# More attention tiles transposed on VectorE, and two steps moved ahead, in a fused top-k attention and GELU MLP kernel

## The chip, the cores and the metric

One core of one Trainium2 chip runs the whole program. The metric is the device time of one execution in microseconds (us), less is better; the median of some runs stands for a kernel. The engines of the core are TensorE (PE, with its weight loads as PEld), VectorE (DVE), ScalarE (ACT), GpSimd (POOL) and SyncE, whose queue (SP) issues the DMAs here. Each runs its own instructions in program order and waits on semaphores for the others.

## The reference

Attention over 8 batches and 8 heads, 576 positions of 64 values, in which each query keeps only its 32 largest scores; then an MLP over the 4608 tokens. All is 32-bit float.

```python
scores = q @ k.transpose(0, 1, 3, 2) / np.sqrt(D)
kth = np.partition(scores, -32, axis=-1)[..., -32:-31]
scores = np.where(scores >= kth, scores, -1e9)
attn = np.exp(scores - scores.max(-1)); attn /= attn.sum(-1) + 1e-9
x = (attn @ v), heads side by side      # 4608 x 512
h = x @ w_in                            # 512 -> 2048
out = (0.5 * h * (1 + erf(h / np.sqrt(2)))) @ w_out
```

## The kernel before, in words

**Items and rings.** The attention is cut into 144 items. An item is 128 query rows of a pair of heads, so its scores are 128 × 1152 (two heads of 576 keys). A batch has 18 items: sixteen main ones (four pairs with four blocks of 128 rows) and two tail items for the last 64 rows of each head. `RINGS` is 36, the items of two batches; a ring of the loop is 36 iterations, and what an item gets is often decided by its number modulo 36. Below, n≡13 means an iteration whose number is 13 modulo 36.

**One iteration.** The loop over n works on several items at once. It issues the scores of n+2 and n+3 (L408, with the last 64 keys as the small matmul L373), the products P·V of item n−3 (`attend`, L742), ScalarE's selection and exponentials of n−1 (`select` L538, `softmax` L550), the transposes of P of n−2 (`transposes`, L657 and L671, copied out of PSUM by L660 and L686), the 32 largest of each row of n on VectorE (`top_k`: rounds of MAX8, L504, and MATCH_REPLACE, L507), and pieces of the MLP, which `room_in(n)` deals out to the iterations: first layer L811, second layer L929 to L967. Order within each engine is the order in which these calls are made.

**The top 32.** MAX8 gives 8 values of a row at a time. To shorten the first rounds, a row of 576 is folded to two halves of 288: the larger of each pair on VectorE (`larger`, L443), the smaller by an integer sum on POOL (`sum_up`, L468) less the larger (`smaller`, L476). Both lie in a tile "lists", of which there are two. The call of `larger(n+1)` stands at the start of iteration n, so on VectorE it follows the end of `top_k(n−1)`.

**From threshold to weights.** When the last MAX8 of item n has run, POOL turns the 32nd value into two biases (`threshold`, L518 and L519), ScalarE selects with the first one (L538, twice) and takes exponentials with the second (L550, twice, which also sums the row). POOL adds 1e-9 to the sums (`add_small`, L531), VectorE takes the reciprocal (`inverse`, L525, called as `last` at the end of the next `top_k`), and POOL multiplies the row by it (`normalise`, L573).

**Two ways to turn P.** P·V needs P with keys on partitions. The common way is nine 128 × 128 transposes on TensorE (L657 once, L671 eight times) and two copies on ScalarE. A *squared* item (`squared(i)`) goes another way: VectorE transposes it in 32 × 32 squares in place (`square_p`, L605, in the middle of the `top_k` two iterations later), SP writes it to DRAM by four DMAs (`write_p`, L615) and reads it back by four others in the turned order (`read_p`, L625). Before the change 66 items are squared: from 27 on, the even ones except 12 modulo 36, most tail items, and the odd ones that are 3, 13 or 25 modulo 36 (`LATER`, `moved(i)`).

**What "moved" brings.** A moved item i is attended at n = i+4 instead of i+3 (`mid`, `mids()`), since the way through DRAM takes longer. Its product uses the pair of PSUM banks "pr", of which there is one, shared with the scores and with the transposes "tp" of L671. `bare` in `room_in` shifts two MLP pieces by one iteration. Where the product's copy into xT (L747, by ScalarE) stands is decided around L1285: for an item in `starts_next` (1 modulo 36) ahead of the exponentials, for the others behind the first of them. Another bank, "z", serves by turns the product "seven" of the second layer (L965, copied by L983 or L986), the tail transposes and last keys ("t_ps", "tp_t").

**ScalarE in an odd iteration**: the two selects L538, a table load and the gelu (L827), the copy of "seven", a table load and the exponentials.

Of the kernel before, what the change touches and what calls it, by code (L numbers as in the profile page):

```python
# [14 lines left out]
def kernel(  # L15
# [19 lines left out]
    nc = tc.nc  # L35
    f32, i32, u32 = mybir.dt.float32, mybir.dt.int32, mybir.dt.uint32
    bf16, i16, u16 = mybir.dt.bfloat16, mybir.dt.int16, mybir.dt.uint16
    AF = mybir.ActivationFunctionType
    ALU = mybir.AluOpType

    B, H, S, D = q.shape
    P = 128
# [20 lines left out]
    work = ctx.enter_context(tc.tile_pool(name="work", bufs=2))  # L63
# [46 lines left out]
    def flush():  # L110
        held[0] = False
        while late_issues:
            late_issues.pop(0)()
        late_issues.extend(later)
        later.clear()
# [142 lines left out]
    for b in range(B):  # L258
# [4 lines left out]
        last = [(b * NP + p, NM) for p in range(0, NP, 2)]  # L263
# [13 lines left out]
    few = [False]  # L277
# [151 lines left out]
    lists_of = {}  # L429
    HS = S // 2  # L430

    def paired(i):

        return PAIRED <= i < N and i not in SINGLE

    def halves_of(i):
        s = S_of[i].rearrange("p (e h n) -> p e h n", e=2, h=2)
        return s[:, :, 0], s[:, :, 1]

    def larger(i):  # L440

        if paired(i):
            nc.vector.tensor_tensor(lists_of[i][:, :, 0], *halves_of(i), op=ALU.max)  # L443

    def into_of(i):

        if i < 2 and i not in into_lists:
            into_lists[i] = work.tile([P, 2, 2, HS], f32, tag="pt", bufs=1, name="into")
        return into_lists.get(i, lists_of[i])
# [3 lines left out]
    def first_lists():  # L453
# [6 lines left out]
        nc.gpsimd.tensor_tensor(both, a.bitcast(i32), top, op=ALU.subtract)  # L460
        nc.gpsimd.tensor_tensor(both, both, b.bitcast(i32), op=ALU.add)

    def sum_up(i):

        if paired(i):
            lists_of[i] = t = work.tile([P, 2, 2, HS], f32, tag="lists", name="lists")
            a, b = halves_of(i)
            nc.gpsimd.tensor_tensor(  # L468
                t[:, :, 1].bitcast(i32), a.bitcast(i32), b.bitcast(i32), op=ALU.add
            )  # L470
# [7 lines left out]
    def top_k(i, last, middle):  # L478


        stat_of[i] = st = {
            "first": work.tile([P, 2, 8], f32, tag="first", name="first"),
        }
        stat = work.tile([P, 4, 2], f32, tag="stat", name="stat")
        st.update((n, stat[:, x]) for x, n in enumerate(("neg", "bias", "den", "rden")))
        top = work.tile([P, 2, 16], f32, tag="top", bufs=1, name="top")
        into = [st["first"]] + [
            top[:, :, 8:16] if r == TOPK // 8 - 1 else top[:, :, 0:8] for r in range(1, TOPK // 8)
        ]
        if paired(i):  # L490
            t = lists_of[i]
            u = into_of(i)
            both = u.rearrange("p e h n -> p e (h n)")
            rounds = [(t[:, :, 0], u[:, :, 0]), (u[:, :, 0], u[:, :, 0])]
            rounds = [(*(rounds[r] if 16 * r < TOPK else (both, both)), x) for r, x in enumerate(into)]
        else:
            s = S_of[i].rearrange("p (e n) -> p e n", e=2)
            t = work.tile([P, 2, S], f32, tag="lists", name="rest")
            rounds = [(s if r == 0 else t, t, x) for r, x in enumerate(into)]
        for r, (src, dst, x) in enumerate(rounds):  # L500
            if 16 * r == TOPK:
                middle()
            for e in range(2):
                nc.vector.max(x[:, e], src[:, e])  # L504
            if r < len(rounds) - 1:
                for e in range(2):
                    nc.vector.match_replace(dst[:, e], x[:, e], src[:, e], LOWEST)  # L507
            if r == len(rounds) - 1:
                last()

        st["kth"] = top[:, :, 15]
# [9 lines left out]
    def inverse(i):  # L521
        if i < 0 or i >= N:
            return
        st = stat_of[i]
        nc.vector.reciprocal(st["rden"], st["den"])  # L525
# [17 lines left out]
    def softmax(i, e):  # L543

        if i < 0 or i >= N:
            return
        st, s = stat_of[i], row(i, e)
        if (i, e) not in selected:
            select(i, e)
        nc.scalar.activation(  # L550
            s, s, func=AF.Exp, bias=st["bias"][:, e : e + 1], scale=1.0,
            accum_out=st["den"][:, e : e + 1],
        )
# [23 lines left out]
    def squared(i):  # L577

        if not SINGLE.stop - 2 < i < N - 2:
            return False  # L580
        if items[i][1] == NM:
            return i % RINGS != RINGS // 2 - 1
        return moved(i) or (i % 2 == 0 and i % RINGS != 12)

    LATER = (3, 13, 25)

    def moved(i):

        return RINGS <= i < N - 8 and i % RINGS in LATER

    def delayed(i):

        return squared(i) and items[i][1] == NM
# [4 lines left out]
    RINGS = 2 * len(items) // B  # L598
    turned = {}

    def square_p(i):

        if squared(i):
            s = S_of[i]
            nc.vector.transpose(s, s)  # L605

    def write_p(i):

        if squared(i):
            turned[i] = d = dram.tile([SQ, NJ + NM, P // SQ, P], f32, tag="turned", name="turned")  # L610
            s = S_of.pop(i).rearrange("p (x j) -> p x j", j=SQ)
            d = d.rearrange("i c k n -> i (c k) n")
            for a in range(P // SQ):
                rows = slice(a * SQ, (a + 1) * SQ)
                nc.sync.dma_start(out=d[:, :, rows], in_=s[rows])  # L615
# [498 lines left out]
    def mlp(n):  # L1114
        for _ in range(n):
            if done[0] >= len(pieces) or pieces[done[0]][0] > ready[0] or left[0] == 0:
                return
            pieces[done[0]][1]()
            done[0] += 1
            left[0] -= 1  # L1120
            if eager[0]:
                run_gelus()
                run_small(9)
# [33 lines left out]
    for pair in range(2):  # L1157
        for piece in transpose_qk(pair, pair == 0):
            piece()
        if pair == 0:  # L1160
            scores(0)
            first_lists()
            scores(1)
            sum_up(1)
# [28 lines left out]
    starts_next = [x + 1 for x in starts]  # L1193
    sums_in = {START + 8 + j: j for j in range(FT // 2)}
    ahead = N + 4
    for n in range(ahead):

        held[0] = n < N and squared(n - 2)
        mid = [i for i in (n - 5, n - 4) if delayed(i) and n % 2 and (i % 2 or i in starts)]
        if moved(n - 4):  # L1200
            mid = [n - 4]
# [9 lines left out]
        def mids():  # L1211
            attend(mid.pop(0))
            if not mid:
                copy_x()
                read_p(n - 3)
                issue_soon()
# [7 lines left out]
        if n > 0:  # L1224
            larger(n + 1)
# [57 lines left out]
            softmax(n - 1, 1)  # L1283
        if few[0]:
            room = ODD if n % 2 else 0  # L1285
            if mid and mid[0] in starts_next:
                mlp(1)
                mids()
                room -= 1
            if n % 2 or not ahead_of_x:  # L1290
                softmax(n - 1, 0)
            if mid:
                mlp(1)
                mids()
                room -= 1
            if n % 2 and ahead_of_x:
                softmax(n - 1, 1)
            mlp(room)
# [35 lines left out]
        mlp(left[0])  # L1334
        run_gelus()
        if n < N:
            top_k(n, lambda: inverse(n - 1), lambda: square_p(n - 2))
            write_p(n - 2)
            flush()
            if n == 0:  # L1340
                larger(1)
        else:
            inverse(n - 1)
        threshold(n)
        if n == 0:
            smaller(1)
        normalise(n - 1)
        sum_up(n + 2)
        if n in sums_in:
            weight_sums(sums_in[n])  # L1350
# [56 lines left out]
```

## Time and profile before

| | |
|---|---|
| median of 3 runs | 1465.61 us (1465.57 to 1466.32) |
| the profiled execution | 1466.12 us, of which its span is 1464.0 |
| TensorE busy | 1444.8 us (99%), 8639 matmuls |
| VectorE busy | 1323.7 us (90%) |
| ScalarE busy | 1060.0 us (72%) |
| POOL busy | 1138.0 us (78%) |
| DMA | 134.13 MB, 92 GB/s on average |

A row of the time line reads: start (us from the start of the span), duration (us), engine, line, operation, tile written <- tiles read, shapes, how many such in a row; in brackets the idle time just before on that engine and what ended it. In the groups stand the total busy time and the mean of one in ns. In the waits stand who waited for whom, the total, how often, and the longest.

### The profile page before, as it was taken

The numbers are of one execution on the slowest core, as the hardware profiler recorded it, in microseconds if no ns is written. First come the engines' busy times: TensorE is split into PE (matmuls) and PEld (weight loads), VectorE is DVE, ScalarE is ACT, GpSimd is POOL, SyncE is SP. The second block draws the span as 40 slices with busy tenths as digits, with TensorE's granted clock in tenths as the row PEclk, the third lists the DMA queues.
The fourth block names the chain that finished last, engine by engine and source line by source line (L and its number), as shares of the span: only waits on it lengthen the run. The fifth ranks groups of instructions, "written<-read, shape, count | busy, mean of one in ns | idle before, by whom it ended". The sixth has DMA issues, their size and how long they took to land. (4 is left out here: it accounts for less than half of the span.)

```text
span 1464.0 us, 26591 instructions
## 1 busy us (share of the span) xinstructions
PE 1444.8 (99%) x8639; PEld 1126.5 (77%) x8639; DVE 1323.7 (90%) x3337; ACT 1060.0 (72%) x1887; POOL 1138.0 (78%) x1290
## 2 busy tenths in 40 slices
PE   8999999999999999999999999999999999999999
PEld 6776677877777777787777778787777777787887
DVE  7999899999999999999999999999999999999701
ACT  7999977876777777767777777776776767677620
POOL 6877667877897879877898878887788887978632
PEclk9999999999999999999999999999999999999999
DMA  7524310045454446455454365455555443643300
GB/s 193 152 87 124 85 48 1 16 96 99 90 113 89 84 91 141 82 112 113 96 100 95 61 116 115 89 114 112 98 100 110 86 84 78 128 99 75 65 15 15
DMA packets 580043, 134.13 MB, mean 92 GB/s; under 512 B 494881, under 2 KB 571457, under 8 KB 579905
## 3 DMA queue, kind: packets, MB, share of 16 engines
q1 hardware_dynamic: 578640, 132.01, 42.6%
q8 instruction: 68, 1.11, 0.3%
q14 instruction: 71, 0.57, 0.1%
q10 hardware_dynamic: 1200, 0.39, 0.1%
q0 software_dynamic: 64, 0.03, 0.0%
HBM read 84.01 MB, written 48.37 MB: 90 GB/s over the span
## 5 line engine op out<-in xcount | busy, mean ns | idle before, releaser
L811 PE MATMUL h_ps<-xT,w_in_sb 128*128 128x256 f32 (+1 forms) x2560 | 533.2, 361 | 0.0
L811 PEld LDWEIGHTS h_ps<-xT,w_in_sb 128*128 128x128 f32 x2560 | 438.2, 190 | 70.3 <-issue 11.3
L504 DVE MAX8 top<-lists 128x8 f32<-128x576 f32 (+1 forms) x792 | 475.0, 638 | 0.0
L507 DVE MATCH_REPLACE8 lists<-top,lists 128x288 f32<-128x288 f32 (+1 forms) x528 | 307.4, 587 | 0.0
L538 ACT ACTIVATE s<-s,stat 128x576 f32<-128x576 f32 x288 | 217.8, 778 | 113.4 <-POOL stat L518 113.2
L573 POOL TENSOR_TENSOR s<-s,stat 128x1152 f32<-128x1152 f32 x135 | 286.3, 2121 | 0.3 <-DVE stat L525 0.3
L550 ACT ACTIVATE s<-s,stat 128x576 f32<-128x576 f32 x288 | 223.8, 780 | 7.6
L468 POOL TENSOR_TENSOR lists<-s 128x576 int32<-128x576 int32 x133 | 189.9, 1427 | 0.0
L476 POOL TENSOR_TENSOR lists<-lists 128x576 int32<-128x576 int32 x132 | 186.1, 1410 | 3.1
L742 PE MATMUL o<-pt,raw_v 128*64 128x256 f32 x1280 | 152.9, 384 | 1.5 <-issue 0.6
L416 ACT ACTIVATE s<-s_ps 128x1024 f32<-128x1024 f32 x127 | 125.0, 1032 | 39.6 <-PE s_ps L408 39.5
L531 POOL TENSOR_SCALAR stat<-stat 128x2 f32<-128x2 f32 x144 | 31.4, 218 | 153.7 <-ACT s L550 147.2
L742 PEld LDWEIGHTS o<-pt,raw_v 128*64 128x64 f32 x1280 | 87.4, 136 | 81.9 <-issue 38.9
L967 PE MATMUL y_ps<-w_out_sb,sum 128*128 128x256 f32 x472 | 140.4, 379 | 0.0
L408 PE MATMUL s_ps<-kt,qm 64*128 64x512 f32 x512 | 129.6, 619 | 0.8 <-ACT s L414 0.8
L827 ACT ACTIVATE g<-h_ps 128x512 f32<-128x512 f32 x144 | 78.2, 595 | 70.3 <-PE h_ps L811 69.7
L967 PE MATMUL y_ps<-w_out_sb,g 128*128 128x256 f32 x480 | 115.8, 381 | 0.0
L507 DVE MATCH_REPLACE8 lists<-first,lists 128x288 f32<-128x288 f32 x264 | 114.1, 437 | 0.0
L443 DVE TENSOR_TENSOR lists<-s 128x576 f32<-128x576 f32 x133 | 109.1, 821 | 4.4 <-ACT s L381 1.8
L504 DVE MAX8 first<-lists 128x8 f32<-128x288 f32 x268 | 106.3, 435 | 0.0
L967 PEld LDWEIGHTS y_ps<-w_out_sb,g 128*128 128x128 f32 x480 | 90.5, 190 | 14.4 <-issue 2.3
L967 PEld LDWEIGHTS y_ps<-w_out_sb,sum 128*128 128x128 f32 x472 | 89.7, 190 | 12.2
(162 smaller groups left out, 2373.4 us busy)
## 6 DMA issues: line engine op xcount, KB each, us to landing
turned<-s SPq DMA_DIRECT2D x264, 144.0 KB, 3.6
pt<-turned SPq DMA_DIRECT2D x264, 144.0 KB, 3.2
raw_v<-in_v_dram SPq DMA_DIRECT2D x64, 128.0 KB, 2.5
raw_q<-in_q_dram SPq DMA_DIRECT2D x112, 72.0 KB, 2.4
raw_k<-in_k_dram SPq DMA_DIRECT2D x112, 72.0 KB, 2.4
out_dram<-y SPq DMA_DIRECT2D x30, 256.0 KB, 3.1
w_out_sb<-in_moe_w_in_dram SPq DMA_DIRECT2D x14, 511.8 KB, 4.9
w_out_sb<-in_moe_w_out_dram SPq DMA_DIRECT2D x10, 511.8 KB, 4.0
```

The lines of the kernel that those rows point to most:

```text
L408: nc.tensor.matmul(s_ps[:, e], lhsT=q_t[rows, :], rhs=kt[rows, main_keys(pair)], start=True, stop=True)
L416: nc.scalar.activation(spread(s, S + TL, SM), s_ps, func=AF.Copy, scale=scale)
L468: nc.gpsimd.tensor_tensor(t[:, :, 1].bitcast(i32), a.bitcast(i32), b.bitcast(i32), op=ALU.add)
L476: nc.gpsimd.tensor_tensor(into_of(i)[:, :, 1].bitcast(i32), both, top, op=ALU.subtract)
L504: nc.vector.max(x[:, e], src[:, e])
L507: nc.vector.match_replace(dst[:, e], x[:, e], src[:, e], LOWEST)
L538: nc.scalar.activation(s, s, func=AF.Prelu, bias=st["neg"][:, e : e + 1], scale=1.0, alpha=STEEP)
L550: nc.scalar.activation(s, s, func=AF.Exp, bias=st["bias"][:, e : e + 1], scale=1.0, accum_out=st["den"][:, e : e + 1],)
L573: nc.gpsimd.tensor_tensor(s, s, wide, op=ALU.mult)
L742: nc.tensor.matmul(o[e * D : (e + 1) * D, 0:n], lhsT=vt[:, j, e, :], rhs=pt[:, e * NJ + j if j < NM else NM, :], start=(j == 0), stop=(j = ...
L811: nc.tensor.matmul(h_tile(u)[:, i, :], lhsT=w_in_sb[:, ko, f * P : (f + 1) * P], rhs=xT[:, ko, c0 : c0 + n], start=(ko == 0), stop=(ko == ...
L967: nc.tensor.matmul(acc[names][:, k], lhsT=lhsT, rhs=rhs, start=(j == 0 and k == 0), stop=(j == FT // 2 - 1 and k == 1),)
```

## The change

Three edits. `LATER` goes from three numbers to six, so that of the odd items those that are 1, 9 and 31 modulo 36 go by squares as well (eight items: 37, 45, 67, 73, 81, 103, 109, 117); since 3 stands first, `LATER[0]` is 3. The copy of the product of an item 3 modulo 36 is put ahead of the exponentials, like that of 1 modulo 36. And at the end of `top_k(n)` VectorE computes `larger(n+2)` ahead of the reciprocal of n−1, where before it came behind it; the tile "lists" is made by whichever comes first, `larger` or `sum_up`. The order of the instructions on TensorE is otherwise kept, but for the nine transposes of each of the eight items, their products, which move one iteration later, and two first-layer pieces around each.

```diff
+    have_larger = set()
+
     def larger(i):
 
-        if paired(i):
-            nc.vector.tensor_tensor(lists_of[i][:, :, 0], *halves_of(i), op=ALU.max)
+        if paired(i) and i not in have_larger:
+            have_larger.add(i)
+            nc.vector.tensor_tensor(lists_for(i)[:, :, 0], *halves_of(i), op=ALU.max)
...
+    def lists_for(i):
+
+        if i not in lists_of:
+            lists_of[i] = work.tile([P, 2, 2, HS], f32, tag="lists", name="lists")
+        return lists_of[i]
+
     def sum_up(i):
 
         if paired(i):
-            lists_of[i] = t = work.tile([P, 2, 2, HS], f32, tag="lists", name="lists")
+            t = lists_for(i)
...
-    LATER = (3, 13, 25)
+    LATER = (3, 1, 9, 13, 25, 31)
...
-            if mid and mid[0] in starts_next:
+            if mid and (mid[0] in starts_next or mid[0] % RINGS == LATER[0]):
                 mlp(1)
                 mids()
                 room -= 1
...
-            top_k(n, lambda: inverse(n - 1), lambda: square_p(n - 2))
+            def last():
+                if few[0]:
+                    larger(n + 2)
+                inverse(n - 1)
+
+            top_k(n, last, lambda: square_p(n - 2))
```

## The prediction, made before the result was known

> **What bounds the kernel now.** I read the page's head and engine sums first, then the windows of two whole rings (36 iterations each), then the waits grouped by what ended them, then the time line of single iterations.
>
> ```profile
> span 1464.0 us, 26591 instructions
> PE 1444.8 (99%) x8639; PEld 1126.5 (77%) x8639; DVE 1323.7 (90%) x3337; ACT 1060.0 (72%) x1887; POOL 1138.0 (78%) x1290
> ```
>
> ```profile
> 362.50:706.20 343.70, 342.00 (x2024) 266.96 (x2023) 331.00 (x838) 250.56 (x452) 285.78 (x322) 1.00 0.50 101
> 706.20:1050.40 344.20, 342.14 (x2025) 267.05 (x2025) 331.10 (x839) 250.53 (x452) 285.75 (x322) 1.00 0.51 101
> ```
>
> The columns are the stretch, its length, then the busy time of PE, PEld, DVE, ACT and POOL. TensorE is busy for 342.1 of 344.2 us at a granted clock of 1.00; VectorE for 331.1. So TensorE sets the time, but VectorE has only 13.1 us of room in a ring, and the waits say what that room is made of:
>
> ```profile
> DVE stat L525 <- POOL stat L531: 55.2, 68, 6.2
> ACT s L538 <- POOL stat L518: 113.2, 43, 6.1
> ```
>
> VectorE idles almost only ahead of its reciprocal (L525), which waits for POOL's small addition L531. And ScalarE waits for VectorE's last MAX8 through POOL's L518 before its two selects. In an odd iteration those selects stand ahead of two table loads, the gelu and the copy of "seven", whose bank the next last-keys matmul on TensorE takes. So TensorE follows VectorE's threshold there with a fixed lag. This iteration, n=43, shows it:
>
> ```profile
> 419.24 0.17 DVE L525 RECIPROCAL stat<-stat 128x2 f32<-128x2 f32 x1 [0.21 <-POOL stat L531]
> 419.29 0.22 POOL L518 TENSOR_SCALAR stat<-top 128x2 f32<-128x2 f32 x1
> 419.54 1.44 ACT L538 ACTIVATE s<-s,stat 128x576 f32<-128x576 f32 x2 [6.11 <-POOL stat L518]
> 423.26 0.38 ACT L986 COPY p<-seven 128x256 f32<-128x256 f32 x1
> 423.70 0.49 PE L373 MATMUL tp_t<-kt,qm 128*128 128x128 f32 x2
> 424.02 0.27 PE L657 MATMUL tp_t<-ident,s 128*128 128x128 f32 x1
> 424.13 0.60 PE L967 MATMUL y_ps<-w_sum,sum 128*128 128x256 f32 x2
> 425.73 0.35 ACT L747 COPY xT<-o 128x256 f32<-128x256 f32 x1
> ```
>
> From threshold to the end of the copy of "seven" go 4.35 us (423.64 − 419.29), and TensorE starts 0.06 us later: no slack. At n=41 (mod 36: 5) and n=73 (mod 1) the copy ends 0.99 and 1.08 us before TensorE comes; at n=59 and 61 (mod 23, 25) TensorE waits for it even now:
>
> ```profile
> 404.31 0.38 ACT L983 COPY y<-seven 128x256 f32<-128x256 f32 x1
> 405.68 0.27 PE L373 MATMUL t_ps<-kt,qm 128*128 128x128 f32 x1
> 710.38 0.38 ACT L986 COPY p<-seven 128x256 f32<-128x256 f32 x1
> 711.84 0.27 PE L373 MATMUL tp_t<-kt,qm 128*128 128x128 f32 x1
> ```
>
> ```profile
> 574.96 1.39 PE L753 MATMUL o<-pt,raw_v 128*64 128x64 f32 x40 [0.27 <-ACT p L986]
> 597.35 0.49 PE L373 MATMUL tp_t<-kt,qm 128*128 128x128 f32 x2 [0.27 <-ACT p L986]
> ```
>
> **The change part by part.** *Squares.* Items 37, 45, 67, 73, 81, 103, 109 and 117 become squared: 1, 9 and 31 of the rings, less 139, which is past the limit.
>
> ```profile
> L605 DVE STREAM_TRANSPOSE s<-s 128x1152 f32<-128x1152 f32 x66 | 89.9, 1362 | 0.0
> L686 ACT COPY pt<-tp 128x1024 f32<-128x1024 f32 x67 | 68.3, 1020 | 38.8 <-PE tp L671 37.8
> 1363.23 0.87 PE tp L671 x8
> ```
>
> Each takes from TensorE eight transposes of 0.87 us together (the chain's row) and the one of L657, 0.11 (424.02 to 424.13): 0.98, in all 8 × 0.98 = 7.8 us. ScalarE loses a 1.02 and a 0.25 us copy, off its path. VectorE gains 8 × 1.36 = 10.9 us. Each also issues four writes and four reads on SP's queue:
>
> ```profile
> pt<-turned SPq DMA_DIRECT2D x264, 144.0 KB, 3.2
> 421.98 2.53 SPq L625 DMA_DIRECT2D pt<-turned  x4
> ```
>
> The item behind each moved one is read only after the moved product, as 40 is at 421.98; its own product comes in the next iteration (9.55 us each, 343.7/36), so the 3.2 us lie under TensorE's work and cost nothing; without that cover they would cost up to 3.2 each, 25.6 in all. SP is otherwise idle here. Two first-layer pieces move by one iteration and cost nothing in sum.
>
> *Product copied early.* At n=43, 79 and 115 the eight L671 wait for L747, which stands behind an exponential (425.73 above):
>
> ```profile
> 426.13 1.09 PE L671 MATMUL tp<-ident,s 128*128 128x128 f32 x8 [0.97 <-ACT xT L747]
> ```
>
> The stall of some 1.14 us (with its weight load) goes: 3 × 1.14 = 3.4. If VectorE took no part, the sum would be −7.8 − 3.4 = −11.2.
>
> *Larger halves first.* In 116 iterations L443 goes ahead of the reciprocal. Where that waits for POOL at the end of ScalarE's exponentials (four places in a ring, as 545.50 below), VectorE gets 0.6 to 0.76 us; where POOL itself is late with L476 (n≡2, 10 and others), L476 and L443 cannot run at once, so I count 0.18. Whether the order costs anything shows in pairs of rows:
>
> ```profile
> 706.40 0.22 POOL L518 TENSOR_SCALAR stat<-top 128x2 f32<-128x2 f32 x1 [0.59 <-DVE stat L525]
> 706.42 0.78 DVE L443 TENSOR_TENSOR lists<-s 128x576 f32<-128x576 f32 x1
> 706.58 0.67 POOL L519 TENSOR_TENSOR stat<-top,first 128x2 f32<-128x2 f32 x1
> ```
>
> ```profile
> 564.46 0.76 DVE L443 TENSOR_TENSOR lists<-s 128x576 f32<-128x576 f32 x1
> 564.51 0.79 POOL L518 TENSOR_SCALAR stat<-top 128x2 f32<-128x2 f32 x1 [0.58 <-DVE stat L525]
> ```
>
> ```profile
> 685.50 2.11 POOL L573 TENSOR_TENSOR s<-s,stat 128x1152 f32<-128x1152 f32 x1
> 685.77 2.45 DVE L443 TENSOR_TENSOR lists<-s 128x576 f32<-128x576 f32 x1 [0.62 <-ACT s L381]
> ```
>
> Where POOL's L518 starts 0.02 us ahead of L443 it takes 0.22 and L519 is held; where L443 starts 0.05 us ahead, L518 takes 0.79; where POOL's L573 is at work, L443 takes 2.45 instead of 0.76. Now the reciprocal's 0.15 us let L518 in first. Without it, L443 starts about 0.15 us ahead of L518 nearly everywhere, and the threshold comes at the end of L443: 0.79 − 0.22 = 0.57 later, less about 0.1 as L443 starts in the reciprocal's place: an estimate of **+0.47 us** on every select, the value of the nearest row; bounds 0 (as at 706.40) and 0.57.
>
> The Trainium skill, "SBUF — State Buffer", section "Who interferes with whom", says that a VectorE instruction with two SBUF inputs and a GpSimd instruction that reads SBUF exclude each other, and that whichever issues first holds the other off entirely. By it every one of the 116 would pay; the rows at 564.46 and 685.77 agree, and 706.42 differs, where the one issued 0.02 us later lost only 0.02.
>
> *How these meet.* TensorE can keep its gain only where VectorE's threshold is not what it waits for. VectorE is set back to TensorE's pace at n≡2 and 10, where POOL's sums wait for the second layer's products:
>
> ```profile
> 725.61 0.17 DVE L525 RECIPROCAL stat<-stat 128x2 f32<-128x2 f32 x1 [1.04 <-POOL stat L531]
> 796.05 0.73 POOL L848 TENSOR_TENSOR sum<-g 128x256 f32<-128x256 f32 x1 [2.12 <-PE y_ps L967]
> 801.35 0.17 DVE L525 RECIPROCAL stat<-stat 128x2 f32<-128x2 f32 x1 [1.68 <-POOL stat L531]
> 545.50 0.17 DVE L525 RECIPROCAL stat<-stat 128x2 f32<-128x2 f32 x1 [1.43 <-POOL stat L531]
> ```
>
> From n≡2 to 8: VectorE has one more transpose and the later threshold, less 0.18 at n≡2 and some 0.25 of the short waits between (0.21 at 419.24): +1.36 + 0.47 − 0.18 − 0.25 = +1.4. TensorE has −0.98. They meet at "seven" of n≡5 and 7: 1.4 + 0.98 = 2.4 us of waiting, part of it put off from 5 to 7 by the slack of 0.99. With the gain of 0.98 and the old stall of 1.14 gone, 2.4 − 0.98 − 1.14 = **+0.3**.
>
> From n≡10 to 13: VectorE +1.36 + 0.47 − 0.18 = +1.65, TensorE −0.98. At n≡13 item 9's product is now copied behind the first exponential, in the pair of banks that the transposes take:
>
> ```profile
> 476.57 0.22 POOL L518 TENSOR_SCALAR stat<-top 128x2 f32<-128x2 f32 x1 [0.58 <-DVE stat L525]
> 482.61 1.04 PE L671 MATMUL tp<-ident,s 128*128 128x128 f32 x8
> 482.93 0.19 ACT L550 ACTIVATION_READ_ACCUMULATOR s<-s,stat 128x1 f32 x1
> ```
>
> Here the copy would begin at 483.02 and end at 483.37 (6.80 after L518; 6.79 at n=43), where TensorE came at 482.61: 0.76 + 1.65 + 0.98 = 3.4 us of waiting, **+2.4** after the gain of 0.98.
>
> From 13 to 25 the rows that wait 0.27 lose their cause in part, since VectorE fills its waits there: **−0.3** (bounds −0.9 and 0). From 25 to 2: −0.98 for item 31, of which the pin at n≡1 (slack 1.08) leaves **−0.1** (bounds −0.98 and +0.5). Sum: 0.3 + 2.4 − 0.3 − 0.1 = +2.3 a ring, in three **+7.0 us**.
>
> The profiled execution took 1466.12 us, 2.1 outside its span; the median of the runs, 1465.61, is 1.6 over the span. 1464.0 + 7.0 + 1.6 is about 1472.5.
>
> **The rivals.** *A, the forecast*: VectorE's threshold sets TensorE's pace. For it: lags with 0.06 and no slack; against it: that the places are few. 1468.5 to 1477, by the bounds of its terms (0.2 to 0.57 of delay, the last two stretches at either end).
>
> *B, TensorE alone sets the time*: 1464.0 − 11.2 + 1.6 = 1454.4. For it: 99% busy, and VectorE's 13.1 us of room a ring against 8 × 1.36 = 10.9 in three. Against it: that room stands ahead of L525, mostly at places other than those where the transposes are put. It decides in favour of B if the tp of n≡13 comes more than 6.8 us after L518, against 6.04 now (482.61 − 476.57) less what TensorE saves.
>
> *C, no delay from L443's order* (L518 still gets through): 0.47 a meeting goes, VectorE keeps its fills, and the sum per ring is −0.5 to 0, about 1464. For it: 706.42, where 0.02 us decided in POOL's favour. Part-way to B the stall at n≡13 shrinks while item 31 keeps its 0.98: 1457 to 1462.
>
> *D, worse*: the pin at n≡1 holds back all of item 31's gain and n≡13's wait carries through to 25, with nothing given back: 3 × (0.3 + 2.4 + 0.5) = 9.6 and more, over 1476. The change not doing what it says: L443 first is issued in all 116 places, so only its benefit can fail, which is C or A.
>
> **How the numbers follow.** A 0.5 (1472.5), C 0.2 (1464), B 0.13 (1454.4), between B and C 0.07, D 0.1. A run of this kernel tells about 0.2% from no change, 2.9 us: faster is under 1462.7. B and the part-way case with a little of C make faster 0.22; C and A's lower edge make same 0.18; the rest of A and D make slower 0.60. The range goes from 1457 to 1477 and leaves out most of B and D. A's own range is 1468.5 to 1477.
>
> **What would show it.** Right: eight L671 that wait for L747 at n≡13 for some 3 us three times (and none at n≡7); "seven" waited for at n≡5 and 7 by 1 to 2 us each; L518 at 0.7 to 0.8 us in most rows. TensorE's busy sum falls by 7.8, VectorE's rises by some 11. B is shown by a span that falls with TensorE's sum; C by L518 at 0.22 behind L443. The forecast is wrong if VectorE's reciprocal still waits as long in a ring as now.

## The result, and the profile after

| | before | changed |
|---|---|---|
| median of 7 runs, us | 1466.0 (1464.96 to 1467.45) | 1470.4 (1469.86 to 1472.59) |
| ratio | | 1.0034, 95% interval 1.0023 to 1.0045 |
| span of the profiled execution | 1464.0 | 1468.4 |

The change makes the kernel 4.4 us slower: on the side of the forecast, whose size was +7.0. The page of the changed kernel, its head and engine sums:

```profile
span 1468.4 us, 26543 instructions
PE 1441.6 (98%) x8567; PEld 1119.6 (76%) x8567; DVE 1337.1 (91%) x3345; ACT 1049.9 (71%) x1871; POOL 1129.4 (77%) x1290
```

The 72 transposes are gone from TensorE (8639 to 8567), and eight instructions more run on VectorE (3337 to 3345), busy for 13.4 us longer. TensorE's share has fallen: it waits. (Its busy sum fell by 3.2 us, not by the 7.8 that the transposes were to save.) Its waits, in total, times, longest (L373 is unmoved, L680 was L671, L756 was L747, L992 and L995 were L983 and L986, L751 was L742):

```profile
PE tp_t L373 <- ACT y L992: 3.5, 3, 1.2
PE tp L680 <- ACT xT L756: 2.9, 3, 1.0
PE tp_t L373 <- ACT p L995: 2.8, 6, 0.6
...
PE t_ps L373 <- ACT y L992: 1.7, 2, 1.2
PE o L751 <- DMA turned<-s: 1.1, 1, 1.1
```

The waits for the copy of "seven" (L992, L995) are new but for the short ones at n=59 and 61. The wait of the transposes for the product's copy has the same total as before, 2.9, and yet is another: it is gone from n≡7 and has come to n≡13. The time line of n=49 shows both, from the threshold (L527, L518 before) on:

```profile
477.93 0.22 POOL L527 TENSOR_SCALAR stat<-top 128x2 f32<-128x2 f32 x1 [0.53 <-DVE top L513]
477.95 0.78 DVE L446 TENSOR_TENSOR lists<-s 128x576 f32<-128x576 f32 x1
...
482.34 0.49 PE L373 MATMUL tp_t<-kt,qm 128*128 128x128 f32 x2 [1.16 <-ACT y L992]
...
484.78 0.33 PE L680 MATMUL tp<-ident,s 128*128 128x128 f32 x1 [0.97 <-ACT xT L756]
```

The threshold stands 1.36 us later than before (477.93 against 476.57), the copy of "seven" behind it begins at 481.91, and TensorE, which had saved its transposes, waits 1.16 us there and 0.97 us once more for the product. At n=41 and 43 it waits for "seven" alone (the bank is "t_ps" at n=41):

```profile
406.22 0.49 PE L373 MATMUL t_ps<-kt,qm 128*128 128x128 f32 x2 [1.17 <-ACT y L992]
...
425.11 0.49 PE L373 MATMUL tp_t<-kt,qm 128*128 128x128 f32 x2 [0.60 <-ACT p L995]
```

How far TensorE is behind the kernel before can be read at the start of one and the same scores matmul (L408) in both traces:

| place (start before, us) | ring 1 | ring 2 | ring 3 |
|---|---|---|---|
| ahead of n≡2 | −0.21 (371.1) | 1.36 (696.9) | 2.20 (1041.1) |
| behind n≡7 | 0.22 (429.8) | 1.65 (772.7) | 2.50 (1116.8) |
| behind n≡13 | 2.24 (524.2) | 3.07 (888.3) | 4.52 (1212.1) |
| behind n≡25 | 2.23 (601.3) | 3.12 (945.5) | 4.57 (1289.0) |
| end of the ring, item 31 done | 1.36 (696.9) | 2.20 (1041.1) | 4.44 (1347.0), no item 31 |

So the loss has one place: the stretch to n≡13 costs 2.0, 1.4 and 2.0 us, and n≡2 to 7 some 0.3 to 0.4; where item 31 is squared 0.9 comes back.

### The profile page after: what moved, and what is told of

It reads as the page before. It is cut to its first block, busy times and chain, and to the rows that moved or that the text cites. A ratio compares the mean times of both kernels' runs of the same rounds, so it can differ in the third digit from the quotient of the medians.

```text
span 1468.4 us, 26543 instructions
## 1 busy us (share of the span) xinstructions
PE 1441.6 (98%) x8567; PEld 1119.6 (76%) x8567; DVE 1337.1 (91%) x3345; ACT 1049.9 (71%) x1871; POOL 1129.4 (77%) x1290
## 5 line engine op out<-in xcount | busy, mean ns | idle before, releaser
L582 POOL TENSOR_TENSOR s<-s,stat 128x1152 f32<-128x1152 f32 x135 | 284.8, 2110 | 8.6 <-DVE stat L534 3.4
L485 POOL TENSOR_TENSOR lists<-lists 128x576 int32<-128x576 int32 x132 | 186.6, 1414 | 3.1
L540 POOL TENSOR_SCALAR stat<-stat 128x2 f32<-128x2 f32 x144 | 44.1, 306 | 164.6 <-ACT s L559 152.6
L751 PE MATMUL o<-pt,raw_v 128*64 128x256 f32 x1280 | 152.9, 384 | 2.5 <-DMA turned<-s 1.1
L751 PEld LDWEIGHTS o<-pt,raw_v 128*64 128x64 f32 x1280 | 87.9, 136 | 79.2 <-issue 38.3
L408 PE MATMUL s_ps<-kt,qm 64*128 64x512 f32 x512 | 129.6, 619 | 0.8 <-ACT s L414 0.8
L446 DVE TENSOR_TENSOR lists<-s 128x576 f32<-128x576 f32 x133 | 106.2, 799 | 17.4 <-ACT s L381 6.0
L614 DVE STREAM_TRANSPOSE s<-s 128x1152 f32<-128x1152 f32 x74 | 101.1, 1366 | 0.0
```

Of the source, the lines that this page charges most:

```text
L408: nc.tensor.matmul(s_ps[:, e], lhsT=q_t[rows, :], rhs=kt[rows, main_keys(pair)], start=True, stop=True)
L485: nc.gpsimd.tensor_tensor(into_of(i)[:, :, 1].bitcast(i32), both, top, op=ALU.subtract)
L582: nc.gpsimd.tensor_tensor(s, s, wide, op=ALU.mult)
L751: nc.tensor.matmul(o[e * D : (e + 1) * D, 0:n], lhsT=vt[:, j, e, :], rhs=pt[:, e * NJ + j if j < NM else NM, :], start=(j == 0), stop=(j = ...
```

## The experiments

Times are the median less that of the kernel before on the same chip (1466.07, 1466.52 and 1466.09 for the three sets). The interval is that of the ratio.

| run | us against before | ratio |
|---|---|---|
| changed kernel | +4.4 | 1.0034 (1.0023 to 1.0045) |
| e1 no new squares | −2.1 | 0.9986 (0.9977 to 0.9994) |
| e2 larger halves behind | +4.7 | 1.0033 (1.0021 to 1.0045) |
| e3 new squares free | −1.2 | 0.999 (0.9981 to 0.9999) |
| e4 early copy for 9 | +2.7 | 1.0019 (1.001 to 1.0028) |
| e6 only 9 | +1.7 | 1.0015 (1.0006 to 1.0024) |
| e8 early copy alone | −4.0 | 0.9974 (0.9963 to 0.9984) |
| e9 free, early copy for 9 | −1.3 | 0.9992 (0.9983 to 1.0001) |
| e10 early copy and 31 | −5.1 | 0.9964 (0.9952 to 0.9976) |
| e11 early copy, 1 and 31 | −0.9 | 0.9994 (0.9985 to 1.0003) |
| e12 the same, free | −5.1 | 0.9966 (0.9953 to 0.9978) |
| e13 early copy, 9 free | 0.0 | 0.9999 (0.999 to 1.0007) |
| e16 early copy, 21 and 31 | +1.4 | 1.0008 (0.9999 to 1.0016) |

**e1: the squares taken out.**

```diff
-    LATER = (3, 1, 9, 13, 25, 31)
+    LATER = (3, 13, 25)
```

> The changed kernel without the eight new squared items: the larger halves ahead of the reciprocal and the early copy stay. Theory P (VectorE's threshold sets TensorE's pace, and the eight transposes on VectorE are what it cannot bear): the stall of 1.14 us at n=43, 79 and 115 goes and little comes back, so 2 to 5 us under the kernel before. Rival O (the new order on VectorE is what costs, since POOL's small instructions are held off while L446 runs): 1 to 5 us above the kernel before, close to the changed kernel.

2.1 us under the kernel before: the loss is the squares'. But the early copy alone gives 4.0 (e8), so the reordering costs 1.9 here.

**e2: the reordering taken out.**

```diff
             def last():
-                if few[0]:
-                    larger(n + 2)
                 inverse(n - 1)
```

> The changed kernel with the larger halves behind the reciprocal again; the eight squares and the early copy stay. Theory P: the transposes cost as before and VectorE can no longer fill its waits for the reciprocal, so 0 to 6 us above the changed kernel (4 to 10 us above the kernel before). Rival O: the delays of POOL's small instructions go, and the time falls to within 2 us of the kernel before or under it.

4.7 us over the kernel before, the same as the changed kernel within the intervals. Rival O falls for the kernel with the squares. What is striking is VectorE's wait for POOL ahead of its reciprocal, in e2 and then in the changed kernel:

```profile
DVE stat L534 <- POOL stat L540: 54.4, 68, 6.2
```

```profile
DVE stat L534 <- POOL stat L540: 29.7, 29, 6.2
```

The reordering takes 25 us off this wait, and the time stays. But most of the 25 us are not won. The idle time ahead of L446 itself (the last but one number of these rows, first e2, then the changed kernel) grows by 13.7 us:

```profile
L446 DVE TENSOR_TENSOR lists<-s 128x576 f32<-128x576 f32 x133 | 105.2, 792 | 3.7 <-ACT s L381 1.3
```

```profile
L446 DVE TENSOR_TENSOR lists<-s 128x576 f32<-128x576 f32 x133 | 106.2, 799 | 17.4 <-ACT s L381 6.0
```

VectorE's busy sum is 7.1 us larger as well (1330.0 in e2, 1337.1). Span less busy sum, its idle time goes from 137.8 to 131.3 us: 6.5 us less, not 25.

**e3: the new squares without VectorE's work.** The kernel leaves the eight transposes on VectorE out, so that eight items of P stay unturned; the rest of their way is kept.

```diff
-        if squared(i):
+        if squared(i) and not (moved(i) and i % RINGS in (1, 9, 31)):
             s = S_of[i]
             nc.vector.transpose(s, s)
```

> The changed kernel without the eight new transposes on VectorE; all else of the squares stays (the way through DRAM, the later products, nine transposes fewer on TensorE each), so eight items of P reach the product unturned. Theory P: with 8 x 1.36 us of VectorE gone TensorE keeps its 7.8 us and the 3.4 us of the early copy, but for a stall behind the product's copy at n=49, 85 and 121 of 1 to 1.5 us each: 5 to 9 us under the kernel before. Rival W (the later product, its pair of PSUM banks and the DMAs are what costs, VectorE's load is not): within 2 us of the changed kernel.

1.2 us under the kernel before, 5.6 under the changed one. VectorE's eight transposes are worth most of what was lost, which W denied; but theory P had 5 to 9 under the kernel before, and it missed: something else holds TensorE too. Of its waits there remain 2.6 us for the product's copy at n≡13, 2.4 for "seven", and this one:

```profile
PE o L751 <- DMA pt<-turned: 1.7, 2, 0.9
```

It is the way through DRAM, which the prediction had put at nothing. A smaller term stands in the rows of a moved product in e3:

```profile
1160.64 1.03 PE L974 MATMUL seven<-w_sum,g 128*128 128x256 f32 x4
1161.51 1.03 PE L976 MATMUL y_ps<-w_out_sb,g 128*128 128x256 f32 x4
1162.46 2.38 PE L751 MATMUL o<-pt,raw_v 128*64 128x256 f32 x20
1164.77 1.13 PE L976 MATMUL y_ps<-w_out_sb,g 128*128 128x256 f32 x4
1165.74 0.59 PE L976 MATMUL y_ps<-w_sum,sum 128*128 128x256 f32 x2
```

Four matmuls take 0.87 us from start to start (1160.64 to 1161.51); the four ahead of the product take 0.95 and the four behind it 0.97. A change between 128*128 and 128*64 so costs about 0.1 us here. A moved product stands alone among 128*128 ones, where an unmoved one follows the scores, which are 64*128; an estimate from these rows is that up to 0.2 of the 0.98 goes back, which leaves about 0.8 for a square. The Trainium skill, "TensorEngine Tiling (Array Packing)", section "Key Properties", says that a change of the tiling mode drains TensorE, without a price; these rows agree with it: they show a loss at the change, of that size.

**e4: the product of 9 copied early too.**

```diff
-            if mid and (mid[0] in starts_next or mid[0] % RINGS == LATER[0]):
+            if mid and (mid[0] in starts_next or mid[0] % RINGS in (3, 9)):
```

> The changed kernel with the product of the items 9 modulo 36 copied ahead of the exponentials too. In the changed kernel TensorE stalls at n=49, 85 and 121 twice: 1.3 us for the copy of seven and 1.14 us for the product's copy. Theory P says that the threshold is only one of the two, so the second stall goes, the first stays, and some of it is met again at the next place: 1 to 3.4 us under the changed kernel, still at or above the kernel before. Rival (the threshold pins everything that follows): no difference from the changed kernel within 1 us.

1.7 us of 4.4 come back. As the theory said, the wait for "seven" at n=49 stays (0.91 here, 1.16 in the changed kernel); and two new ones appear behind it, shorter, 0.38 us ahead of the tail scores (L423) and 0.55 ahead of the next product. This is the one for "seven":

```profile
482.36 0.49 PE L373 MATMUL tp_t<-kt,qm 128*128 128x128 f32 x2 [0.91 <-ACT y L992]
```

**e6: 9 alone.**

```diff
-    LATER = (3, 1, 9, 13, 25, 31)
+    LATER = (3, 9, 13, 25)
```

> The changed kernel with 9 modulo 36 as the only new squares (items 45, 81, 117; the reordering and the early copy stay). Theory N (the loss sits in the stretch from n=10 to 13 modulo 36, where TensorE meets the late threshold and then the product's copy, 2.0 us a ring): 2 to 5 us above the kernel before, against 2.1 under it without new squares. Rival S (each of the eight costs alike, 6.5 us over eight): about 0.3 us above the kernel before, within 1 us.

1.7 us over the kernel before, so 3.8 over e1: three squares at 9 cost 1.3 us each. That is nearer to N than to S (0.3), but below N's range: the rest of the loss is elsewhere, as e11 shows for 1 modulo 36.

**e8: the early copy alone**, the kernel before with this one edit:

```diff
-            if mid and mid[0] in starts_next:
+            if mid and (mid[0] in starts_next or mid[0] % RINGS == LATER[0]):
```

> The kernel before with the early copy of the products 3 modulo 36 and nothing else. It takes a stall of 1.14 us off TensorE in each of three rings. Theory P: most of it stays, 2.4 to 3.4 us under the kernel before, and the reordering, which the run without new squares has besides (2.1 under), is worth nothing or up to 1 us less than nothing. Rival F (the reordering is what gave those 2.1 us): 0 to 1.5 us under the kernel before.

4.0 us under the kernel before, all that three stalls of 1.14 can give and 0.6 more, so past theory P's 3.4; F falls. The 1.9 us that the reordering costs in e1 are more than the 1 that P allowed. The transposes of n=43, at 424.79, wait for nothing.

**e9: e3 and e4 together**, the new squares free and 9 copied early.

> The changed kernel without the eight new transposes on VectorE (those items of P reach the product unturned), and with the products 9 modulo 36 copied early. Theory: nothing but the switches of tile shape around the moved products (some 0.2 us each) and a wait of 0.5 us for the scores in each ring is then left of the price, so 8 x 0.77 + 3 x 1.14 less about 3 x 0.6 gives 6 to 8 us under the kernel before. Rival W (something else that a moved product brings eats the gain): 1 to 3.5 us under it.

1.3 us under: the theory's 6 to 8 is missed and W holds; the early copy for 9, worth 1.7 us in e4, adds nothing to e3. The rows name what takes it, at n=50:

```profile
470.11 1.37 DVE L614 STREAM_TRANSPOSE s<-s 128x1152 f32<-128x1152 f32 x1
470.69 2.54 SPq L634 DMA_DIRECT2D pt<-turned  x4
473.27 2.22 SPq L130 DMA_DIRECT2D raw_q<-in_q_dram  x4
475.60 3.43 SPq L624 DMA_DIRECT2D turned<-s  x4
481.84 2.54 SPq L634 DMA_DIRECT2D pt<-turned  x4
...
487.40 0.87 PE L751 MATMUL o<-pt,raw_v 128*64 128x256 f32 x6 [1.82 <-DMA pt<-turned]
```

Item 46, an even one that was squared before the change too, was not back from DRAM when TensorE came. Its reads follow its writes (475.60, then 481.84). But its writes do not follow VectorE at once: VectorE was done with it at 471.48 (470.11 and 1.37), and the writes stand 4.1 us later, behind four reads of the item before and four loads of "raw_q" on the same queue. So what holds TensorE here is in part the order on SP's queue, and not VectorE's pace alone. That is read from the rows; no run changes the order on that queue. The prediction called SP otherwise idle; at this place it is not.

**e10: the early copy and 31, no reordering.**

```diff
-    LATER = (3, 1, 9, 13, 25, 31)
+    LATER = (3, 13, 25, 31)
...
-                if few[0]:
-                    larger(n + 2)
                 inverse(n - 1)
```

> The kernel before with the early copy and two new squares, items 67 and 103 (31 modulo 36); no reordering. Theory: in the changed kernel the stretch of these two kept 0.75 us each, where VectorE has room; so 3 to 5 us under the kernel before, the fastest so far. Rival (VectorE's 1.36 us come back at the next thresholds, n=5 and 7 modulo 36): no better than the early copy alone within 0.7 us.

5.1 us under the kernel before, the fastest of the kernels that compute everything, just past the theory's edge. 1.1 us beyond e8 for two squares is less than the 0.75 us each that the theory wanted, and not clear of the noise by itself; the traces show 0.71 and 0.11 us at the two places.

**e11: 1 besides.**

```diff
-    LATER = (3, 13, 25, 31)
+    LATER = (3, 1, 13, 25, 31)
```

> The kernel before with the early copy and the new squares 1 and 31 modulo 36 (37, 67, 73, 103, 109), no reordering. Accounting so far, beside the kernel before: early copy -3.8, 31 -1.3, and what is left of the changed kernel's +4.4 for 1 modulo 36 after 9 (+3.9) and the reordering (+1.2 to +1.7) is about +4. If the parts add up, 0 to 1.5 us under the kernel before. Rival (1 modulo 36 hurts only together with 9 and the reordering): 4 us or more under it.

0.9 us under. The parts add up: the three squares at 1 cost 4.2 us beside e10, 1.4 each. TensorE waits for "seven" at n=41 and 43, as in the changed kernel, by 0.70 and 0.67 us.

**e12: e11 with the five transposes left out on VectorE**, by e3's edit for 1 and 31.

> The same kernel without the five new transposes on VectorE (those items of P reach the product unturned). Theory: for 1 and 31 modulo 36 VectorE's 1.36 us is the only price, so TensorE keeps 5 x 0.77 us beside the early copy's 3.8: 6 to 8 us under the kernel before. Rival (the later product and the way through DRAM cost as they did in the run with all eight free): 2 to 4.5 us under it.

5.1 us under, between the two expectations. VectorE's five transposes cost 4.2 us (e11 to e12), and TensorE's waits for "seven" ahead of L373 show where: they sum to 5.1 us in e11 and to 0.9 in e12. Five squares that cost VectorE nothing give 1.1 us beyond the early copy, where TensorE alone would give 3.9 (five times 0.78). Most of the missing part shows as the wait for the way through DRAM again, which has 0.9 us in e8:

```profile
PE o L751 <- DMA pt<-turned: 3.9, 6, 1.4
```

**e13: 9 without VectorE's work, no reordering**, `LATER = (3, 9, 13, 25)` and e3's edit for 9.

> The kernel before with the early copy and the new squares 9 modulo 36, without their three transposes on VectorE (unturned P), no reordering. Theory: for 9 modulo 36 there is a second price, the transposes of n=13 modulo 36 that wait for the product's copy (1.14 us a ring), which eats the 0.77: 1.5 to 3.5 us under the kernel before, no better than the early copy alone. Rival (VectorE's 1.36 us is all that 9 costs): 5 to 6.5 us under it.

0.0: worse by 1.5 us than the theory's edge, and far from the rival. Even a free square at 9 costs 1.3 us beside e8. Its product's copy stands behind the exponential, and the transposes of n=49 wait for it (481.77 to 482.12). The moved product ahead of them starts late too, for no cause that the profile names, and the next product waits 0.30 us for its reads:

```profile
475.68 2.38 PE L751 MATMUL o<-pt,raw_v 128*64 128x256 f32 x20 [0.37 <-issue]
...
482.18 1.09 PE L680 MATMUL tp<-ident,s 128*128 128x128 f32 x8 [0.98 <-ACT xT L756]
```

That is 0.37 + 0.98 + 0.30 = 1.65 us by the profile's ends, more than the 0.8 that a square saves. That 9 has this second price is as the theory said; its size was not.

**e16: 21 instead of 1 and 9, where VectorE waits anyway.** `LATER = (3, 13, 21, 25, 31)`, no reordering.

> The kernel before with the early copy and the new squares 31 and 21 modulo 36 (21 instead of 1 and 9), no reordering. VectorE turns item 21 at n=23 modulo 36, where its reciprocal waits 1.06 us for POOL anyway and the threshold waits with it. Theory: a transpose put where VectorE waits costs nothing at the next threshold, so TensorE keeps 0.5 to 0.77 us a ring: 5.5 to 7.5 us under the kernel before, the fastest. Rival (the pins of n=23 and 25, with no slack, take it back, or the product's later place does): 1 to 5 us under it, no better than 31 alone.

1.4 us over the kernel before, 6.5 over e10: the theory falls, and its rival's 1 to 5 us under the kernel before is missed as well. At n=61 the same two waits stand in a row as at n=49 in the changed kernel, and at n=71, where item 31's product is copied, the transposes wait too, as they do at n=107 and nowhere in e10:

```profile
596.11 0.49 PE L373 MATMUL tp_t<-kt,qm 128*128 128x128 f32 x2 [1.02 <-ACT p L995]
598.55 1.09 PE L680 MATMUL tp<-ident,s 128*128 128x128 f32 x8 [0.97 <-ACT xT L756]
...
694.55 1.09 PE L680 MATMUL tp<-ident,s 128*128 128x128 f32 x8 [0.98 <-ACT xT L756]
```

With 21 squared, what 31 gave in e10 is so lost too.

## Why the prediction was right, and where it was not

**The sum by parts.** From e8, e10, e11, e2 and the changed kernel, each one edit further: early copy −4.0; 31 −1.1 (two squares); 1 +4.2 (three); 9 +5.6 (three); reordering −0.3; together +4.4. Each step is a difference of two runs with about 1.6 us of interval on either side, so the sign of the reordering's step is not shown (the spans of the two profiled executions, 1467.8 and 1468.4, have it the other way). The parts also depend on each other: without 1 and 31 the three squares at 9 cost 3.8 (e1 to e6).

**The mechanism held, the size was in part luck.** TensorE follows VectorE's threshold through the copy of "seven": e11 and e12 differ by nothing but five VectorE transposes, by 4.2 us, 0.8 each, and by as much in TensorE's waits for "seven". The time lies within A's own range because three wrong terms, below, partly cancel: n≡10 to 13 and 25 to 2 were put too dear, 13 to 25 too cheap. B, TensorE alone, is out: even without VectorE's work the gain does not come (e3, e9, e12).

**Early copy.** Forecast −3.4, measured −4.0; and no wait of the transposes at n≡7, as named.

**n≡2 to 8.** Forecast +0.3, measured +0.43, +0.29, +0.30. The waits for "seven" at n=41 and 43 are 1.17 and 0.60, and no longer than 0.60 in the later rings; 1 to 2 each were named.

**n≡10 to 13.** Forecast +2.4, measured 2.0, 1.4 and 2.0 (in the second a wait of the kernel before went as well). The step had one wait of 3.4 us for the product's copy; there were two, 1.16 for "seven" and 0.97 for the copy. "Seven" came first and was overlooked at this place: the prediction worked out its slack for n≡5, 7, 23 and 25, not for 13. Once TensorE has waited there, the copy behind the exponential is only a fixed distance away.

**13 to 25 and 25 to 2.** Forecast −0.3 and −0.1, measured 0.0 and −0.9. The waits of 0.27 at n=59 and 61 did not lose their cause: they are 0.27 and 0.32. The second term was mis-sized most; it and n≡13 take 3.4 us off the +7.0, and the first puts 1.0 back. Item 31's gain was kept, by the rows below because VectorE paid next to nothing for it. The prediction showed L443 at 685.77, held behind POOL's L573 for 2.45 us after a wait of 0.62 for ScalarE's copy of the last keys; it did not ask whether the change would part them. At that place of the changed kernel, and of e10, which has no reordering:

```profile
688.71 0.78 DVE L446 TENSOR_TENSOR lists<-s 128x576 f32<-128x576 f32 x1
```

```profile
685.33 0.78 DVE L446 TENSOR_TENSOR lists<-s 128x576 f32<-128x576 f32 x1
```

Squaring 31 lets ScalarE copy those keys earlier, L446 is through before L582 (L573) begins, and 1.7 us come back to VectorE, and the wait besides, against 1.36 for the transpose. That these two make the difference between 31 and the others is argued from the rows; no run parts them.

**The reordering's step failed as it was put.** "L443 starts about 0.15 us ahead of L518 nearly everywhere" is not so. At 477.93 and 477.95 POOL is first by 0.02 us, much as before the change (476.57 and 476.60). L443 does not take the reciprocal's place: the reciprocal used to start while the last MAX8 was ending (476.42, which is 0.15 ahead of L518), L443 starts 0.02 behind L518. So L518 is held off where POOL itself comes late to it, in 22 of the 118 iterations from n=26 on over 0.45 us (4 before), and L531 in 26 (none before). Here POOL comes to L527 (L518) behind L540 (L531), at n=43:

```profile
420.08 0.76 DVE L446 TENSOR_TENSOR lists<-s 128x576 f32<-128x576 f32 x1
...
420.32 0.59 POOL L527 TENSOR_SCALAR stat<-top 128x2 f32<-128x2 f32 x1
```

"Nearly everywhere" was wrong, then. But the sum used the delay at two meetings, and at the first it is there: at n≡5 and 7, in all three rings, L527 ends 0.94 us after the last MAX8, where L518 ended 0.47 to 0.51 us after it, close to the estimate of 0.47 for the difference. At the second, n≡13, it is not: both end 0.30 us after it.

What the order costs elsewhere was not foreseen. From L518 to the next item's first MAX8 go 0.73 us before (476.57 to 477.30) and 0.80 after (477.93 to 478.73) at n=49: the reciprocal no longer hides under the last MAX8. And at n≡2 the prediction gave VectorE 0.18 us and put the price on POOL at nothing. These rows are of e1:

```profile
379.31 1.28 DVE L446 TENSOR_TENSOR lists<-s 128x576 f32<-128x576 f32 x1
379.93 1.93 POOL L485 TENSOR_TENSOR lists<-lists 128x576 int32<-128x576 int32 x1
...
391.90 0.19 PEld L408 LDWEIGHTS s_ps<-kt,qm 64*128 64x128 f32 x2 [0.97 <-ACT pt L695]
```

And these of e8, which has no reordering:

```profile
379.89 1.42 POOL L476 TENSOR_TENSOR lists<-lists 128x576 int32<-128x576 int32 x1
...
391.35 0.19 PEld L408 LDWEIGHTS s_ps<-kt,qm 64*128 64x128 f32 x2 [0.48 <-ACT pt L686]
```

L446, moved ahead, meets POOL's L485 (L476), which takes 1.93 us instead of 1.42. The threshold comes at 382.23 instead of 381.69, ScalarE's copy L695 (L686) ends at 391.85 instead of 391.30, and the scores on TensorE, whose weights wait for it, start 0.38 us later (391.91 against 391.53). Against e8, e1 loses 0.3 to 0.4 us at such scores six times, at n≡4 and 12 of each ring, 2.3 us in all; shorter waits elsewhere give some of it back, for the two spans differ by 1.5 (1461.8 and 1460.3).

**DMAs at no cost.** The cover was there in the kernel before, but for one wait of 0.2 us. In the changed one TensorE waits for them twice, 1.07 and 0.56 us:

```profile
747.10 1.26 PE L751 MATMUL o<-pt,raw_v 128*64 128x256 f32 x9 [1.07 <-DMA turned<-s]
```

In e9 and e12, where the threshold holds TensorE back less, this wait takes most of the gain: 3.7 us in e9 and 3.9 in e12.

**What stays open.** Why the reordering's price of 1.9 us without squares (e8 to e1) does not show with them (e2), though with them L485 is held at n≡2 in the first ring only; how much of the waits for DMA is the order on SP's queue and how much VectorE; and whether 31's 1.1 us (e10) would be met again: e10's interval overlaps that of e8.

## What to carry to other kernels

An engine at 99% is not free to gain when another engine at 90% gives it its pace at a few places: look for the places where the lag between the two has no slack (here 0.06 us), follow the work moved from one to the other as far as each of them, and expect the gain to come back as a wait there. A filled slot is worth nothing unless what stands behind it is waited for, and a wait that shrinks need not be time won: VectorE's wait for POOL lost 25 us, its idle time as a whole only 6.5, and the time did not move. When several edits come together, run each alone: one line of this change, the early copy, makes the kernel 4.0 us faster, and the rest hid it.

## What the runs showed of the hardware

In e6's profiled execution (1469.70 us, where the shortest of its eleven took 1467.94) the granted clock is 0.50 in the 3.4 us that follow the two waits at n=49, which end at 480.95 and 483.39; in the stretches on either side it is 1.00 (the third column from the right):

```profile
480.00:483.50 3.50, 1.57 (x8) 1.12 (x9) 3.50 (x10) 3.47 (x8) 3.42 (x5) 1.00 0.29 86
483.50:486.90 3.40, 3.40 (x13) 3.04 (x14) 3.14 (x6) 1.94 (x5) 3.24 (x6) 0.50 0.36 91
486.90:490.00 3.10, 3.10 (x25) 1.55 (x25) 3.10 (x13) 1.03 (x2) 3.10 (x3) 1.00 0.00 0
```

Half of 3.4 us is 1.7 us, about the distance between that execution and the shortest. TensorE was busy for 1.57 of the 3.50 us ahead of it. The waits that a change adds may so cost more than their length in some executions; but the same two waits in the changed kernel's profile were followed by a full clock, so that they are the cause is not shown.
